# Attention with the scores turned round and their row maxima carried as operand rows

## The chip, the cores and the metric

One NeuronCore of a Trainium2 chip runs the whole kernel. The metric is the device time of one execution, in microseconds (us). The engines have their own instruction queues and run at the same time: TensorE (PE, and PEld for its weight loads), VectorE (DVE), ScalarE (ACT), GpSimd (POOL) and SyncE (SP), which here issues all the transfers (DMA).

## The reference, cut to what matters

Four batches of twelve heads, 448 tokens, head width 64. q and k are normalised by their root mean square; then comes softmax attention; its output, 1792 tokens of width 768, goes through a soft mixture of eight experts and then a gated product. All data are float32.

```python
q_n, k_n = (rmsnorm(q, g_q), rmsnorm(k, g_k))          # (4, 12, 448, 64)
scores = scale * np.matmul(q_n, k_n.transpose(0, 1, 3, 2))
scores = scores - np.max(scores, axis=-1, keepdims=True)
attn = np.exp(scores)
attn = attn / (np.sum(attn, axis=-1, keepdims=True) + 1e-09)
return np.matmul(attn, v).astype(np.float32)
# then: x = soft mixture of experts (phi, w1, w2) of x;  out = (x @ w_a) * (x @ w_b) @ w_out
```

## The kernel before

The kernel has three stages. Stage 1 is the attention, with the mixture's routing logits for each batch done between its steps. Stage 2 streams the weights of the eight experts, and stage 3 the gated product's weights and the final products. Weights travel in units of 1536 KB: nine of the fifty are loaded during stage 1, seven more as stage 1's buffers come free, the rest as stage 2 and 3 use them up.

Stage 1 goes over 24 *pairs* of heads (two heads fill the 128 partitions). For each pair:

- `load_qk`, `load_v`: three transfers from HBM. `square` (two a pair, on POOL except for the first pairs), `sumsq` (DVE) and `rsqrt` give the reciprocal roots: a logarithm and an exponential on ACT, then three small DVE steps (lines 288 to 292) that refine them. These steps have all their operands in SBUF. `normalise` (POOL) multiplies.
- `emit_T`: eight PE transposes put q and k with the head width on the partitions. ACT copies them out rounded to the short form (`et[:, 0]`, `et[:, 1]`, the high parts) and DVE subtracts to get the low parts.
- `emit_Z`: six transfers from SBUF to SBUF stack high and low parts of one head on 128 partitions, as `z`, so that two matmuls give a product of nearly full precision. There are four `z` tiles, one a head, so the tiles of one head come free as soon as that head's four steps are done.
- Eight *steps*, one for each head and each chunk `c` of 112 queries: `score` (two matmuls over `z`, 448 keys wide, queries on the partitions, then a DVE maximum over the keys, line 360), `expo` (ACT exponential with that maximum as its bias, and the sum over the keys as its accumulator, read out by a second instruction), `ptrans` (four PE transposes that put the keys on the partitions, line 382, and a copy out on ACT, line 388, or DVE, line 386).
- A pair later, `av`: four times two heads' matmuls of `pt` with `v`, accumulated in the PSUM tile `psv`; `spread` and `bcast` (a POOL copy, four PE transposes and an ACT copy) lay the reciprocal sums out over the head width, and `finish` multiplies.

The order of stage 1 is written by hand: a loop of 24 pairs times 8 steps, in which `score` runs two steps ahead and `expo` one. `moe_tasks` (routing logits and accumulation, per batch) are handed out one at a time in steps 3, 6 and 7. Only DVE's order is left to the framework's scheduler in stage 1. The weight units go in after `emit_Z` in step 6 of every second pair from the sixth on. `warm` puts dummy matmuls on PE while it would be idle.

Of the kernel before, what the change touches and what calls it, by code (L numbers as in the profile page):

```python
# [32 lines left out]
def kernel(  # L33
# [33 lines left out]
    P1_ENGINES = {ET.PE, ET.Activation, ET.Pool, ET.SP}  # L67
# [6 lines left out]
    W0 = 22  # L74
    WE = 7
# [73 lines left out]
    def tok_softmax(s, tp, pt):  # L149

        ps = pt("pslt")[0:P, 0:128]
        for c in range(NC):
            pe.matmul(
                ps[:, c * 32:(c + 1) * 32], s["l4"][:, c * P:(c + 1) * P], i4, start=True, stop=True
            )
        p3 = ps.rearrange("p (c s) -> p c s", s=32)
        m = tp.tile([P, 2, 4], F32, tag="cm", name="cm", bufs=1)
        ct = tp.tile([P, 4, 32], F32, tag="ct", name="ct", bufs=1)
        bc = lambda a: a.unsqueeze(2).to_broadcast([P, 4, 32])
        dve.tensor_reduce(out=m[:, 0, :], in_=p3, axis=AX.X, op=ALU.max)  # L160
        dve.tensor_tensor(out=ct, in0=p3, in1=bc(m[:, 0, :]), op=ALU.subtract)
        act.activation(out=ct, in_=ct, func=AF.Exp)
        dve.tensor_reduce(out=m[:, 1, :], in_=ct, axis=AX.X, op=ALU.add)
        dve.tensor_scalar(out=m[:, 1, :], in0=m[:, 1, :], scalar1=EPS, scalar2=None, op0=ALU.add)
        dve.reciprocal(out=m[:, 1, :], in_=m[:, 1, :])
        dve.tensor_tensor(out=ct, in0=ct, in1=bc(m[:, 1, :]), op=ALU.mult)
        s["ct"] = ct

    def tok_transpose(s, b, tp, pt):

        ps = pt("psct")[0:64, 0:S]
        c2 = tp.tile([P, 4, 2, 32], F32, tag="c2", name="c2", bufs=1)
        dve.tensor_copy(out=c2, in_=s["ct"].unsqueeze(2).to_broadcast([P, 4, 2, 32]))
        for c in range(NC):
            pe.transpose(
                ps[:, c * P:(c + 1) * P], c2[:, c].rearrange("p a s -> p (a s)"), ident[0:P, 0:P]
            )
        act.activation(out=cT[:, b, :], in_=ps, func=AF.Copy)
        dve.tensor_tensor(
            out=cT[32:64, b, :], in0=ps[32:64, :], in1=cT[32:64, b, :].bitcast(F32), op=ALU.subtract  # L180
        )
# [9 lines left out]
    with ExitStack() as c1:  # L191
# [4 lines left out]
        ep = c1.enter_context(tc.tile_pool(name="ep", bufs=1))  # L196
        one = c1.enter_context(tc.tile_pool(name="one", bufs=1))
        sqp = c1.enter_context(tc.tile_pool(name="sqp", bufs=2))
        one_ = c1.enter_context(tc.tile_pool(name="one_", bufs=1))
        pp = c1.enter_context(tc.tile_pool(name="pp", bufs=2))  # L200
        ptp = [c1.enter_context(tc.tile_pool(name="ptp0", bufs=2))]
        vp = c1.enter_context(tc.tile_pool(name="vp", bufs=2))
        sm = c1.enter_context(tc.tile_pool(name="sm", bufs=2))
        ptp.append(c1.enter_context(tc.tile_pool(name="ptp1", bufs=2)))
        ps_s = c1.enter_context(tc.tile_pool(name="ps_s", bufs=3, space=PSUM))
        ps_p = c1.enter_context(tc.tile_pool(name="ps_p", bufs=2, space=PSUM))
        ps_v = c1.enter_context(tc.tile_pool(name="ps_v", bufs=1, space=PSUM))
        ps_m = c1.enter_context(tc.tile_pool(name="ps_m", bufs=2, space=PSUM))
        EVAC_DVE = (1, 5)
        T0A, T0B, T0Z = 5, 6, 6  # L210
        TA, TB, TZ = 4, 5, 6

        NZ = 4
        zt = {(2 * NPAIR + i) % NZ: (one if i < 2 else one_).tile([128, 3, S], F32R, name=f"z{i}") for i in range(NZ)}

        qk_t, n_t, v_t, rinv_t, ssq_t, e_t, pt_t, av_t, xT_t = {}, {}, {}, {}, {}, {}, {}, {}, {}
        ps_of, p_of, nm_of, den_t, bc_t = {}, {}, {}, {}, {}
        NSTEP = 8 * NPAIR

        def load_qk(p):  # L220
            if p >= NPAIR:
                return
            b, hp = divmod(p, HP)
            t = qk_sb[0:P, p % 3 * 1024:(p % 3 + 1) * 1024].rearrange("p (i h x) -> p i h x", i=2, h=2)
            for i, src in enumerate((q, k)):
                sp.dma_start(out=t[:, i], in_=src[b, 2 * hp:2 * hp + 2].rearrange("h (p c) d -> p h (c d)", c=NC))
            qk_t[p] = t

        def load_v(p):
            if p >= NPAIR:  # L230
                return
            b, hp = divmod(p, HP)
            src = v[b, 2 * hp:2 * hp + 2].rearrange("h (p c) d -> p h c d", c=NC)
            if p < NPAIR - 1:
                t = vp.tile([P, 2, NC, D], F32, tag="v", name=f"v{p}")
                sp.dma_start(out=t, in_=src)
                v_t[p] = [t[:, hd] for hd in range(2)]
            else:
                x = tk.tile([128, S], F32, tag="l4", name="v23a", bufs=1)[0:P, 0:NC * D]
                y = tk.tile([P, 4, 2, 32], F32, tag="c2", name="v23b", bufs=1)  # L240
                v_t[p] = x.rearrange("p (c d) -> p c d", d=D), y.rearrange("p c (a e) s -> p c (a e s)", a=2)
                for hd in range(2):
                    sp.dma_start(out=v_t[p][hd], in_=src[:, hd])

        sq_t = {}

        def square(p, i, eng=None):
            if p >= NPAIR:
                return
            sq = sqp.tile([P, 512], F32, tag="sq", name="sq")  # L250
# [5 lines left out]
            sq_t[p, i] = sq  # L256

        def sumsq(p, i):
            if p >= NPAIR:
                return  # L260
# [6 lines left out]
        small = []  # L267

        def tick(n=1):
            for _ in range(n):  # L270
                if small:
                    small.pop(0)[1]()

        def rsqrt(p):

            if p >= NPAIR:
                return  # L280
            x = ssq_t.pop(p).rearrange("p a c -> p (a c)")
            y = sm.tile([P, 2, 8], F32, tag="rinv", name=f"rinv{p}", bufs=3)
            yf = y.rearrange("p a c -> p (a c)")
            t = sm.tile([P, 16], F32, tag="nt", name="nt", bufs=2)
            rinv_t[p] = y
            act.activation(out=t, in_=x, func=AF.Ln, bias=ssq_eps[0:P])
            act.activation(out=yf, in_=t, func=AF.Exp, scale=-0.5)
            small.append((p, lambda: dve.scalar_tensor_tensor(
                out=t, in0=yf, scalar=-0.5, in1=yf, op0=ALU.mult, op1=ALU.mult)))
            small.append((p, lambda: dve.scalar_tensor_tensor(  # L290
                out=t, in0=x, scalar=D * 1e-6, in1=t, op0=ALU.add, op1=ALU.mult)))
            small.append((p, lambda: dve.scalar_tensor_tensor(
                out=yf, in0=t, scalar=1.5, in1=yf, op0=ALU.add, op1=ALU.mult)))

        def normalise(p, eng=None):
            if p >= NPAIR:
                return
            assert not any(x[0] == p for x in small)
            n_t[p] = npp.tile([P, 2, NC, 2, D], F32, tag="n", name=f"n{p}")
            for i in range(2):  # L300
# [4 lines left out]
                        [P, 2, NC, D]  # L305
                    ),
                    op=ALU.mult,
                )
            qk_t.pop(p)

        def emit_T(p, i):
# [911 lines left out]
```

## Time and profile before

| | us |
|---|---|
| median of three runs | 589.34 (588.32 to 589.79) |
| the profiled execution, its own time | 591.54 |
| its span, first to last instruction | 589.6 |
| mean granted clock of TensorE | 0.985 of full speed |

A row of a profile gives the engine, the line of the kernel, the operation, the tiles written and read, and times. A timeline row begins with the start and the duration in us. Durations of matmuls contain the way through the array, so for the throughput of PE the reader should look at the distance between starts.

### The profile page before, as it was taken

How to read it: one execution, taken by the hardware profiler on the slowest of the kernel's cores; microseconds unless marked ns; L12 is line 12 of the kernel's file. 1: busy time of each engine (PE TensorE's matmuls, PEld its weight loads, DVE VectorE, ACT ScalarE, POOL GpSimd, SP SyncE). 2: the span in 40 equal slices, each digit the busy share in tenths (PEclk: the TensorE clock that was granted, in tenths of full speed). 3: DMA queues.
4: the chain of work that ended last, by engine and by line, in shares of the span. 5: the costliest groups of instructions: out<-in, count | busy, mean ns of one | idle time of the engine just before them, and what ended most of it. 6: DMA issues, size and time to landing. Idle time of an engine off the chain costs nothing.

```text
span 589.6 us, 10977 instructions
## 1 busy us (share of the span) xinstructions
PE 555.9 (94%) x3982; PEld 367.2 (62%) x3982; DVE 350.7 (59%) x703; ACT 360.3 (61%) x845; POOL 114.1 (19%) x136
## 2 busy tenths in 40 slices
PE   5889999999999999999999999888999999999997
PEld 5756555566665565655656545333675665689996
DVE  5777777768787677786677522122248878742211
ACT  4577787787787787877868720111279889442210
POOL 1233443333343433333110000001100000200000
PEclk8798999999999999999999999999999999999999
DMA  7956577797877978697769688999999991002332
GB/s 177 221 137 145 142 167 166 192 266 203 206 226 170 265 169 242 164 270 159 219 167 282 245 342 343 430 425 427 423 422 423 425 424 63 1 28 80 97 91 82
DMA packets 39574, 134.51 MB, mean 228 GB/s; under 512 B 5857, under 2 KB 25313, under 8 KB 33121
## 3 DMA queue, kind: packets, MB, share of 16 engines
q1 hardware_dynamic: 39520, 133.81, 72.0%
q8 instruction: 32, 0.52, 0.4%
q14 instruction: 22, 0.17, 0.1%
HBM read 95.26 MB, written 5.51 MB: 171 GB/s over the span
## 4 chain that ended last, share of the span: by engine, by line
PE 76%; DMA 8%; DVE 5%; ACT 4%; SPq 2%; issue 2%; ACTq 0%; DVEq 0%
PE psv L396 12%; PE pspt L382 12%; PE pss L358 6%; PE pss L359 5%; DMA z<-e 5%; PE psM L938 4%; PE psh L697 4%; PE pso L1138 3%; PE pso L1140 3%; PE pso L1139 3%; PE psS L721 3%; PE pst L325 3%; DMA wu_w<-in_moe_w_dram 2%; PE psS L938 2%; PE psx L509 2%
## 5 line engine op out<-in xcount | busy, mean ns | idle before, releaser
L360 DVE TENSOR_REDUCE nmx<-pss 112x1 f32<-112x448 f32 x192 | 118.6, 620 | 41.9 <-PE pss L359 41.5
L382 PEld LDWEIGHTS pspt<-ident,p 112*112 112x112 f32 x768 | 81.3, 135 | 79.7 <-ACT pt L388 28.9
L369 ACT ACTIVATE p<-pss,nmx 112x448 f32<-112x448 f32 x192 | 123.8, 645 | 10.1 <-DVE nmx L360 7.2
L382 PE MATMUL pspt<-ident,p 112*112 112x112 f32 x768 | 110.9, 267 | 2.9 <-ACT p L369 2.8
L388 ACT COPY pt<-pspt 112x448 f32<-112x448 f32 x144 | 76.9, 534 | 27.6 <-PE pspt L382 26.1
L396 PE MATMUL psv<-pt,v 112*64 112x448 f32 x368 | 90.3, 569 | 0.0
L358 PE MATMUL pss<-z 128*112 128x448 f32 x192 | 85.8, 447 | 0.0
L301 POOL TENSOR_TENSOR n<-xw,rinv 112x512 f32<-112x512 f32 x46 | 47.1, 1044 | 177.0 <-PE pst L325 112.1
L359 PE MATMUL pss<-z 128*112 128x448 f32 x192 | 70.9, 369 | 0.0
L386 DVE COPY pt<-pspt 112x448 f32<-112x448 f32 x48 | 29.9, 623 | 20.7 <-PE pspt L382 20.7
L255 POOL TENSOR_TENSOR sq<-xw 112x512 f32<-112x512 f32 x40 | 40.9, 1042 | 4.9 <-DMA xw<-in_q_dram 4.8
L369 ACT ACTIVATION_READ_ACCUMULATOR p<-pss,nmx 112x1 f32 x192 | 40.0, 208 | 0.0
L1138 PE MATMUL pso<-Mh,t 128*128 128x384 f32 x112 | 38.1, 340 | 0.5 <-DVE Ml L967 0.5
L358 PEld LDWEIGHTS pss<-z 128*112 128x112 f32 x192 | 34.4, 179 | 6.7 <-issue 5.8
L1140 PE MATMUL pso<-Mh,t 128*128 128x384 f32 x112 | 37.8, 337 | 0.0
L1139 PE MATMUL pso<-Ml,t 128*128 128x384 f32 x112 | 37.8, 337 | 0.0
L325 PE MATMUL pst<-ident,n 112*128 112x112 f32 x192 | 27.1, 267 | 11.2 <-ACT rd L427 6.0
L1157 DVE COPY ot<-pso 128x384 f32<-128x384 f32 (+1 forms) x14 | 7.6, 544 | 49.9 <-PE pso L1142 49.9
L396 PEld LDWEIGHTS psv<-pt,v 112*64 112x64 f32 x368 | 18.3, 135 | 29.6 <-issue 22.5
L359 PEld LDWEIGHTS pss<-z 128*112 128x112 f32 x192 | 34.5, 180 | 0.7 <-issue 0.6
L938 PE MATMUL psM<-w,G 128*128 128x512 f32 x64 | 33.8, 610 | 0.8 <-DVE G L901 0.8
L263 DVE TENSOR_REDUCE ssq<-sq 112x8 f32<-112x512 f32 x48 | 32.4, 677 | 2.7 <-ACT sq L253 2.3
(177 smaller groups left out, 878.0 us busy)
## 6 DMA issues: line engine op xcount, KB each, us to landing
wu_w<-in_moe_w_dram SPq DMA_DIRECT2D x38, 1536.0 KB, 13.5
z<-e SPq DMA_DIRECT2D x48, 336.0 KB, 4.6
z<-e SPq DMA_DIRECT2D x48, 224.0 KB, 4.4
r<-in_moe_w_dram SPq DMA_DIRECT2D x7, 1536.0 KB, 8.4
xw<-in_moe_w_dram SPq DMA_DIRECT2D x4, 1536.0 KB, 15.2
xw<-in_q_dram SPq DMA_DIRECT2D x24, 224.0 KB, 4.4
xw<-in_k_dram SPq DMA_DIRECT2D x24, 224.0 KB, 4.0
z<-e SPq DMA_DIRECT2D x48, 112.0 KB, 4.4
```

The source lines that it names most:

```text
L301: (eng if eng and i == 0 else pool).tensor_tensor(out=n_t[p][:, i].rearrange("p c h d -> p h c d"), in0=qk_t[p][:, i].rearrange("p h (c d) ...
L358: pe.matmul(ps, x, z[:, 1, :], start=True, stop=False)
L359: pe.matmul(ps, x, z[:, 2, :], start=False, stop=True)
L360: dve.tensor_reduce(out=nm_of[n // 8][:, h % 2, c:c + 1], in_=ps, axis=AX.X, op=ALU.max, negate=True)
L369: act.activation(out=t, in_=ps_of.pop(n), func=AF.Exp, bias=nm_of[n // 8][:, h % 2, c:c + 1], accum_out=den_t[n // 8][:, h % 2, c:c + 1],)
L382: pe.transpose(ps[:, kc * P:(kc + 1) * P], src[:, kc * P:(kc + 1) * P], ident[0:P, 0:P])
L388: act.copy(out=o, in_=i)
L396: pe.matmul(av_t[p][hd * D:(hd + 1) * D, 0:S], v_t[p][hd][:, kc, :], pt_t[2 * p + hd][:, kc, :], start=(kc == 0), stop=(kc == NC - 1),)
L938: pe.matmul(o, G[:, r], W[:, c], start=st, stop=sp_)
L1138: pe.matmul(o, ch[:, m], Mh[:, m, c], start=(m == 0), stop=False)
L1139: pe.matmul(o, ch[:, m], Ml[:, m, c], start=False, stop=False)
L1140: pe.matmul(o, cl[:, m], Mh[:, m, c], start=False, stop=False)
```

## The change

Only stage 1 changes.

- **Scores are transposed.** `score(p, kc, hd)` now puts 112 keys on the partitions and the 448 queries along the row, so the exponential's output is already what `av` needs. `ptrans` and its copies are gone, and so is the read of the accumulator.
- **The maxima come from one pass of their own.** `peak(p, c)` multiplies only the high parts, straight from the tile `e`, one matmul a head on its own 64 partitions, both heads into a two-bank PSUM tile; `peak_out` takes both heads' maxima in one DVE instruction over 896 columns. `rows(p)` transposes the maxima (four transposes of two columns) and `rows_out` (ACT) writes them into rows 64 and 65 of `z`'s fourth plane. The second matmul of `score` runs over 66 rows, and a row of ones (`fill_ones`, once) makes it add the maxima. The exponential then needs no bias.
- **The sums come from the exponentials.** `addup` on POOL adds the four key chunks of both heads (three additions of 896 columns a pair), `den` multiplies them with a matrix of ones (two float32 matmuls), `den_ln`, `den_exp` (ACT) and `den_test`, `den_step` (DVE) invert, and `finish` multiplies. `rden`, `spread` and `bcast` go.
- **Small operands in PSUM.** `root` writes one of two copies of its result, and `newton` its intermediate, into the unused columns 448 and up of the PSUM bank in which `av` accumulates (`bank`, `spare_ps`); `tok_softmax` keeps its four sums there too.
- **Squares shared.** One of the two squares of each pair goes from POOL to ACT (`SQ_ACT`).
- **Split operands of two pairs in turn.** `e` gets two buffers; `z` becomes two tiles of one whole pair each, in place of four of one head. Their number of transfers stays at six a pair, with the same bytes.
- **The order comes from a planner.** Every operation gets a cost, a due time (`p * T0 + OFF[kind]`), its dependencies and the buffers that it takes and gives; a list scheduler works out the order of all five engines. DVE's order in stage 1 is now fixed by it as well. The planner holds a transfer pair `Z` to 2.2 us of issue for a head and 4.0 us to land.

```diff
-    P1_ENGINES = {ET.PE, ET.Activation, ET.Pool, ET.SP}
+    P1_ENGINES = {ET.PE, ET.Activation, ET.Pool, ET.SP, ET.DVE}
+    SQ_ACT = (1,)
+    NPT, T0, MSTEP, WU0, WUS, MF, = 5, 11.5, 3.2, 4, 2, 13
...
-        ep = c1.enter_context(tc.tile_pool(name="ep", bufs=1))
+        ep = c1.enter_context(tc.tile_pool(name="ep", bufs=2))
...
+        zt = [zp[i].tile([128, 2, 4, S], F32R, name=f"z{i}") for i in range(2)]
+        bank = ps_v.tile([128, 512], F32, name="psv")
+        spare_ps = lambda n, w: bank[0:P, S + n:S + n + w]
...
+        def root(p):
             t = sm.tile([P, 16], F32, tag="nt", name="nt", bufs=2)
+            act.activation(out=t, in_=ssq_t[p].rearrange("p a c -> p (a c)"), func=AF.Ln, bias=ssq_eps[0:P])
+            act.activation(out=spare_ps(0, 16), in_=t, func=AF.Exp, scale=-0.5)
+            act.activation(out=t, in_=t, func=AF.Exp, scale=-0.5)
...
+            if s == 0:
+                dve.scalar_tensor_tensor(out=t, in0=spare_ps(0, 16), scalar=-0.5, in1=y, op0=ALU.mult, op1=ALU.mult)
...
+        def stack(p, hd):
+            z = zt[p % 2][:, hd].bitcast(F32)
+            src = e_t[p][hd * D:(hd + 1) * D].bitcast(F32)
+            sp.dma_start(out=z[0:D, 0:3], in_=src[:, QH:KL + 1])
+            sp.dma_start(out=z[D:128, 0:2], in_=src[:, QL:KH + 1:2])
+            sp.dma_start(out=z[0:D, 3], in_=src[:, QH])
...
+        def peak(p, c):
+            for hd in range(2):
+                r = slice(hd * D, (hd + 1) * D)
+                pe.matmul(ps[:, hd], et[r, QH, c * P:(c + 1) * P], et[r, KH, :], start=True, stop=True)
+        def peak_out(p, c):
+            dve.tensor_reduce(out=nm_t[p][:, c, :], in_=ps_of[p, "x"], axis=AX.X, op=ALU.max, negate=True)
...
+        def score(p, kc, hd):
+            pe.matmul(ps, z[:, 1, c], z[:, 0, :], start=True, stop=False)
+            pe.matmul(ps, z[0:66, 2, c], z[0:66, 3, :], start=False, stop=True)
+        def expo(p, kc, hd):
+            act.activation(out=pt_t[p, kc][:, hd, :], in_=ps_of.pop((p, kc, hd)), func=AF.Exp)
+        def addup(p, kc):
+            pool.tensor_tensor(
+                out=sum_t[p], in0=pt_t[p, 0] if kc == 1 else sum_t[p], in1=pt_t[p, kc], op=ALU.add
+            )
...
+        lim = {"qk": 3, "v": 2, "sq": 2, "n": 1, "m": 2, "e": 2, "z": 2, "x": 1, "nm": 2, "s": 3, "pt": NPT, "sum": 1,
...
+                op("SP", 2.2, o("Z", hd), ("Z", p, hd), lambda hd=hd: stack(p, hd), [("L", p, 0), ("L", p, 1)] + ([("Z", p, 0)] if hd else []), () if hd else ("z",))
+                op(None, 4.0, 0, ("z", p, hd), None, [("Z", p, hd)])
...
+                    op("PE", 0.44, o("S", x), ("S", p, kc, hd), lambda kc=kc, hd=hd: score(p, kc, hd),
+                       [("RW", p), ("z", p, hd)], ("s",), (("z", ("Z", p, 0)),) if (kc, hd) == (NC - 1, 1) else ())
...
+            op("SP", 0.6, (WU0 + WUS * x) * T0, ("wu", x), lambda x=x: load_unit(
+                None if x < NRING else 0 if x == NRING else extra),
+               [("S", WU0 + WUS * x, 0, 0)] + ([("wu", x - 1)] if x else []))
```

## Rows read from the trace of the kernel before

**Rows 1.** The page: busy time of PE, and the slices of PE and DMA.

```profile
PE 555.9 (94%) x3982; PEld 367.2 (62%) x3982; DVE 350.7 (59%) x703; ACT 360.3 (61%) x845; POOL 114.1 (19%) x136
...
PE   5889999999999999999999999888999999999997
...
DMA  7956577797877978697769688999999991002332
```

**Rows 2.** Busy time by stretch; at the end PE clock, DMA share, GB/s.

```profile
75.00:102.00 27.00, 25.30 (x163) 15.15 (x163) 19.07 (x42) 21.23 (x60) 10.80 (x12) 1.00 0.70 164
...
130.00:157.00 27.00, 26.61 (x180) 16.67 (x180) 21.60 (x51) 21.60 (x61) 9.35 (x10) 1.00 0.83 215
...
347.00:356.00 9.00, 8.80 (x66) 6.05 (x67) 3.63 (x10) 2.49 (x7) 0.56 (x2) 1.00 0.79 304
356.00:500.00 144.00, 134.49 (x1305) 79.36 (x1304) 68.75 (x119) 75.28 (x93) 7.03 (x13) 0.99 0.92 383
```

**Rows 3.** The tile z: durations min/median/max, first and last start; its transfers.

```profile
L358 PE MATMUL pss<-z x192: 363/437/717, 20.3 to 335.7; 128*112 128x448 f32 x192
...
DMA to landing us min/median/max: 3.4/4.4/6.8
```

**Rows 4.** Timeline of PE: two steps of one pair, and the first scores.

```profile
20.80 0.36 PE L358 MATMUL pss<-z 128*112 128x448 f32 x1
...
21.00 0.37 PE L359 MATMUL pss<-z 128*112 128x448 f32 x1
...
247.03 0.43 PE L358 MATMUL pss<-z 128*112 128x448 f32 x1
247.31 0.37 PE L359 MATMUL pss<-z 128*112 128x448 f32 x1
247.60 0.97 PE L396 MATMUL psv<-pt,v 112*64 112x448 f32 x4
248.51 0.60 PE L382 MATMUL pspt<-ident,p 112*112 112x112 f32 x4
248.87 0.43 PE L358 MATMUL pss<-z 128*112 128x448 f32 x1
249.15 0.36 PE L359 MATMUL pss<-z 128*112 128x448 f32 x1
249.35 0.55 PE L382 MATMUL pspt<-ident,p 112*112 112x112 f32 x4
249.66 0.44 PE L358 MATMUL pss<-z 128*112 128x448 f32 x1
```

**Rows 5.** Groups of the page: count, busy us, mean ns, idle before.

```profile
L360 DVE TENSOR_REDUCE nmx<-pss 112x1 f32<-112x448 f32 x192 | 118.6, 620 | 41.9 <-PE pss L359 41.5
...
L388 ACT COPY pt<-pspt 112x448 f32<-112x448 f32 x144 | 76.9, 534 | 27.6 <-PE pspt L382 26.1
...
L255 POOL TENSOR_TENSOR sq<-xw 112x512 f32<-112x512 f32 x40 | 40.9, 1042 | 4.9 <-DMA xw<-in_q_dram 4.8
```

**Rows 6.** SP's queue: a weight unit, and one pair's six stacking transfers.

```profile
141.98 0.60 SPq L139 DMA_DIRECT2D wu_w<-in_moe_w_dram  x1
...
150.49 0.47 SPq L343 DMA_DIRECT2D z<-e  x1
...
154.55 1.53 SPq L345 DMA_DIRECT2D z<-e  x1
```

**Rows 7.** Timeline: a small DVE step beside POOL's multiplications, and one alone.

```profile
17.34 0.17 DVE L288 SCALAR_TENSOR_TENSOR nt<-rinv 112x16 f32<-112x16 f32 x1
...
18.70 2.05 POOL L301 TENSOR_TENSOR n<-xw,rinv 112x512 f32<-112x512 f32 x2 [5.08 <-DVE rinv L292]
...
19.75 1.03 DVE L288 SCALAR_TENSOR_TENSOR nt<-rinv 112x16 f32<-112x16 f32 x1 [0.68 <-ACT rinv L287]
```

**Rows 8.** Timeline: the last pair's finish, and the product that opens stage 2.

```profile
346.37 0.62 DVE L437 TENSOR_TENSOR xT<-psv,rd 128x448 f32<-128x448 f32 x1 [6.27 <-PE psv L396]
...
356.01 1.42 PE L687 MATMUL psst<-wsel,acc 128*128 128x32 f32 x12
```

More of the change, by code (lines that the diff above doesn't have):

```diff
@@ L147, in release @@
             load_unit(p)
[L149 to L154, printed above, removed]
-            )
[L156 to L167, printed above, removed]
@@ L295, in normalise @@
[L295 to L300, printed above, removed]
-                (eng if eng and i == 0 else pool).tensor_tensor(
-                    out=n_t[p][:, i].rearrange("p c h d -> p h c d"),
-                    in0=qk_t[p][:, i].rearrange("p h (c d) -> p h c d", d=D),
-                    in1=rinv_t[p][:, i, :].rearrange("p (h c) -> p h c", h=2).unsqueeze(3).to_broadcast(
-                        [P, 2, NC, D]
-                    ),
-                    op=ALU.mult,
-                )
-            qk_t.pop(p)
@@ new lines, in den, with den_ln, den_exp @@
+        def den(p):
+            ps = ps_of[p, "d"] = ps_m.tile([128, 512], F32, tag="m", name="psden")[:, 0:S]
+            for hd in range(2):
+                pe.matmul(ps[hd * D:(hd + 1) * D], ones, sum_t[p][:, hd, :], start=True, stop=True)
+        def den_ln(p):
+            rd_t[p] = sm.tile([128, S], F32, tag="rd", name="rd", bufs=1)
+            act.activation(out=rd_t[p], in_=ps_of[p, "d"], func=AF.Ln, bias=eps)
+        def den_exp(p):
+            act.activation(out=rd_t[p], in_=rd_t[p], func=AF.Exp, scale=-1.0)
@@ new lines, in xt_copy, with accum @@
+            def xt_copy(c, h):
+                x = s["xs", c, h]
+                if h == 1 and c >= 2:
+                    dve.tensor_copy(out=x, in_=s["x", c, h])
+                else:
+                    act.copy(out=x, in_=s["x", c, h])
+                s["x", c, h] = x
+            def accum(h):
+                ps = s["a", h] = mt("psacc")[:, 0:HD]
+                for c in range(NC):
+                    pe.matmul(ps[c * 32:(c + 1) * 32, :], s["et"][:, c, :], s["x", c, h], start=True, stop=True)
@@ new lines @@
+        order, start, end = plan()
+        free, tail = 0.0, max(start[names["S", NPAIR - 1, x, 1]] for x in range(NC))
+        ps_w = []
+        for i in order:
+            if ops[i][0] == "PE":
+                gap = start[i] - free
+                if free and gap > 0.8 and start[i] <= start[names["S", 0, 0, 0]]:
+                    warm(ps_of["w"], int(WF * gap / 0.22))
+                elif gap > 0.8 and start[i] > tail + 4:
+                    if not ps_w:
+                        ps_w.append(ps_x.tile([128, 2, 512], F32, tag="x", name="warm")[:, 0])
+                    warm(ps_w[0], int(WF * gap / 0.22))
+                free = end[i]
+            if ops[i][3]:
+                ops[i][3]()
```

759 lines of the change are left out of this document (401 added, 358 removed).

## The prediction

> **What bounds the kernel now.** I read the page first: PE is busy for 94% of the span, and its slices stand at 8 or 9 from the third to the last, while the slices of DMA are near 9 only from the 25th to the 33rd [rows 1]. Then the busy times by stretch. In a stretch of the attention PE fills 25.3 to 26.6 of 27 us at full clock, ACT and DVE 19 to 22, POOL about 10, and the 16 DMA engines 70% without weight units and 83% with them. From 356 to 500 us the DMA moves 383 GB/s at a share of 92%: there the kernel waits for weights [rows 2]. So stage 1 is set by PE and stage 2 by transfers that start to run without a break once the first expert frees its weights. In stage 1 only nine units go in, and seven more while it ends; these sixteen do not depend on how long it lasts. What stage 1 gains is therefore given on, us for us, as long as its last buffers come free in the same order against its end; the DMA share of 79% from 347 to 356 us [rows 2] says that a few us of delay of one unit find room.
>
> Third, the pace. The first score starts at 20.3 us, the last at 335.7 [rows 3]; with 0.6 us for its own two matmuls, 24 pairs take 316 us, 13.17 us a pair, the mixture's tasks included. Fourth, PE's timeline, by starts. Two steps take 2.63 us, 247.03 to 249.66: a score 0.57 before `av` and 0.48 before transposes, `av` 0.91, four transposes 0.36 and 0.31 [rows 4]. Four such rounds are 10.5 us a pair; two `emit_T` and `bcast`, three sets of four transposes like these, make 1.0, and the rest to 13.17, 1.65 us, is the mixture and waiting. I put the waiting at 0.4.
>
> **The change on PE, a pair.** It takes away 4 × (0.36 + 0.31) = 2.68 us of `ptrans` and 0.33 of `bcast` [rows 4]. Scores now come in twos with one passage to and from float32 work instead of two. Back to back, matmuls of a score start 0.20 apart, and 0.27 to 0.29 beside other work [rows 4]; two scores then cost 0.28 + 0.20 + 0.20 + 0.29 = 0.97 against 1.05, so 0.3 us less for four rounds. Together 3.3 us go.
>
> It adds `rows`, four transposes, 0.36; `den`, two float32 matmuls of the width of one `av`, 0.91 [rows 4]; and the peaks, which no row shows. A peak of one chunk is two matmuls of 448 columns, each of which would take 0.20 alone [rows 4]. Below: both heads together take the time of one, 0.20. Above: one after the other with a passage on both sides, 0.28 + 0.29. I take 0.30, since the two heads use different halves of the partitions and write different banks, as the two heads of `av` use different halves of the output: four of those matmuls in 0.91 [rows 4]. Four chunks are 1.2 us, between 0.8 and 2.3. The sum added is 2.47, and PE's work falls by 0.86 us a pair, between 1.26 less and 0.24 more.
>
> The Trainium skill (TensorEngine Tiling (Array Packing), Key Properties) says that tiles of the array run independently, and also that a change of the tiling mode drains the array; by the first half a chunk of peaks would cost the lower bound, by the second nearer the upper. No run here shows row halves.
>
> **The other engines, a pair.** DVE loses eight maxima (118.6/24 = 4.9 us), and gains four over twice the columns. Twice 0.62 is the upper bound and 0.62 the lower [rows 5]; I take 1.1, 4.4 in all. It also gains `den_test` and `den_step`, two passes like a maximum, 1.2 us, and loses a third of the copies. It stays under its present 21.5/27 × 13.2 = 10.5 us a pair [rows 2]. ACT loses six copies of 0.53 (76.9/24 = 3.2 us) [rows 5] and eight accumulator reads, and gains a square, `rows_out`, `den_ln` and `den_exp`, four passes of about that length: it falls. POOL loses a square, 1.04, and the copy of `spread`, and gains three additions of 896 columns. By the square of 512 columns one is 1.04 × 896/512 = 1.82 [rows 5]: 5.5 us more, 8.7 in all, from about 4.6 [rows 2]. None of the three becomes the bound by its sum; their cover is that PE has more than 11 us to do.
>
> DMA's bytes stay. Its 0.70 × 13.17 = 9.2 us a pair without units, and 10.9 with [rows 2], stand in a shorter pair: 87% of 12.5 us. That is below the 92% of stage 2 but no longer far.
>
> The small steps in PSUM: with both operands in SBUF such a step took 0.17 us alone and 1.03 beside a POOL multiplication [rows 7]. Three a pair, on an engine that is not the bound, are worth nothing by themselves; with POOL twice as busy they would have begun to cost, and the move buys that off.
>
> **Waits.** The orders that matter are PE's. New ones: four times a maximum behind a peak (one two-bank buffer), the maxima behind `rows` and ACT's `rows_out` ahead of a pair's scores, the sum chain (addition, `den`, two ACT passes, two DVE passes) ahead of `finish`, which frees the bank for the next pair's `av`. Each has the better part of a pair to run in. The waits of before on the copies out of `pspt` (27.6 us idle on ACT alone [rows 5]) go. The tightest new one is `z`. Before, one head's tile was free after half a pair; now both heads' six transfers can start only when the last score two pairs back is done, and must land before the first score of their pair, one pair later. On SP they take 150.49 to 156.1, and the last lands 4.4 us after its start at 154.55 (median): 8.5 us [rows 3, 6]. A weight unit, 1.57 MB at 383 GB/s, is 4.1 us more [rows 2]. Its due time puts it, in every second pair from the fifth on, between the first head's transfers and the second's; SP also carries q, k and v behind them. That makes 12.6 us, just the length of a pair, and PE stands still for up to 1 us in those eight pairs. I allow 0.2 us a pair over the present waits for this and the rest: 13.17 − 0.86 + 0.19 = 12.5 us a pair.
>
> **The ends.** At the start the chain to the first score gets longer: the four peaks and maxima one behind the other, 4 × (0.3 + 1.1 + 0.3 for two hand-overs), `rows` and `rows_out`, about 8.5 us, beside the stacking transfers, which took the same 8.5. Filling the ones costs ACT four passes of 0.5 while the first q arrives. I take 1.5 us later. At the end, the last score to the last `finish` took 346.99 − 336.3 = 10.7 us [rows 3, 8]; now it is an exponential, an addition, `den`, two ACT and three DVE passes, 0.53 + 1.82 + 0.91 + 1.06 + 1.86 and seven hand-overs of 0.2, 7.6 us. I take 2.5 us less, as PE also has the mixture's first product in there. From there to the product that opens stage 2, 9 us [rows 8], the chain is the same.
>
> **The sum.** 24 × (13.17 − 12.5) = 16.1, less 1.5, plus 2.5: 17 us. The profiled execution would go from 591.54 to 574.5; it stands 2.2 us above the median of the runs, so the time would be 589.34 − 17 = 572.3 us.
>
> **The rivals.** First, the waits go and the peaks of two heads do run together: PE's 12.77 less 1.26 is 11.5, DMA's 10.9 does not let every second pair below about 11.8, and I put the pair at 12.0: 24 × 1.17 + 1 = 29 us, 560 us. For it speaks that PE is nearly without gaps now [rows 2]; against it, that this was a fixed alternation and the new order holds only as well as its costs.
>
> Second, `z` arrives late in most pairs, not only in those with a unit: v, q and k of 672 KB go ahead of it, and the pair settles at 13.0. It gives 24 × 0.17 + 1 = 5 us, 584 us. Against it, their place on SP is now behind `z`.
>
> Third, the shared bank, the one that ends slower. `root` and the three `newton` steps touch the bank of `av`. If accesses by different engines to one bank are kept apart, a step waits for the `av` in progress (0.97 us [rows 4]), and the next `av` on PE, with every score behind it, waits for the step, which stands on DVE behind a maximum of 1.1 us. One such wait a pair is about 1.1 us: 13.4 to 13.6 a pair, 24 × 0.4 − 1 = 9 us more, 598 us. It decides from 0.9 us a pair, where it eats what PE saves. For it: four touches within about 1.5 us, and an `av` about every 3 us, so half of the pairs meet one. Against: a wait on DVE costs only when PE comes up to it in order. The Trainium skill (PSUM — Partial Sum Buffer, PSUM bank collisions raise a hardware error) asks just this, to guard by bank and quadrant and not by address; no row of before shows two engines in one bank of stage 1.
>
> Fourth, the saving is used up by waits of all kinds, each small: no change, 589 us.
>
> **How the numbers follow.** Forecast 0.46 (564 to 580), first rival 0.20, second 0.14, third 0.14, fourth 0.06. A measurement here can tell about 0.3%, 1.8 us, from no change. Faster: 0.46 + 0.20 + 0.14 = 0.80, less 0.03 for second-rival cases that end at nothing, 0.77; same 0.06; slower 0.17. The range goes from 558, just under the first rival, to 591; it leaves out the third and the fastest part of the first.
>
> **What will show it.** Right: scores over about 300 us from start to start, two peaks' starts under 0.05 us apart, no gap of PE at the first score of a pair beyond 1 us, DVE below PE, `wu` followed by a late `z` at most. Wrong: PE's weight loads idle on `z` (second rival), on a `newton` step (third), or on a maximum; a maximum of 896 columns well over 1.1 us; additions on POOL near 2.3 us, which would bring POOL past 10 us a pair and the sum chain onto the path; or a stage 2 that begins earlier and still ends at the old time, since a buffer of stage 1 came free late.

## The result, and the profile after

The changed kernel takes 586.60 us (median of 10 runs, 584.11 to 597.99) beside 590.73 for the kernel before on the same chip (10 runs, 588.32 to 592.53). The ratio is 0.9915, with a 95% interval of 0.989 to 0.9941: about 5 us faster, where 17 were forecast. Some kernels below scatter by several per cent from run to run, with a lower mean clock in the longer runs (here 0.990 at 584.11 us and 0.964 at 597.99), so ratios are made from the runs of each kernel that lie near its fastest.

The profiled execution took 587.84 us with a span of 586.1. First the page: PE's busy time, and the slices of PE, of its granted clock and of DMA.

```profile
PE 557.8 (95%) x3564; PEld 326.8 (56%) x3564; DVE 333.9 (57%) x556; ACT 319.1 (54%) x607; POOL 231.4 (39%) x167
...
PE   8799999999999899999999999898999999999997
...
PEclk9999999999999599999999998999999999999999
DMA  6598699969899378999684869999999991002332
```

Beside [rows 1], PE issues 418 matmuls less and is busy for about 2 us more. One slice of the clock, the 14th, stands at 5; POOL has doubled. Then the stretches of [rows 2], with three of four microseconds around that slice. The columns are the length and the busy time of PE, PEld, DVE, ACT and POOL, then the granted clock, DMA's share and its GB/s; the share counts transfers by where they start, so it can pass 1.

```profile
75.00:102.00 27.00, 26.25 (x128) 11.77 (x127) 21.45 (x37) 20.09 (x44) 21.56 (x16) 1.00 1.05 259
130.00:157.00 27.00, 26.86 (x147) 12.94 (x145) 21.54 (x36) 19.28 (x41) 19.58 (x13) 1.00 0.95 230
188.00:192.00 4.00, 1.77 (x12) 0.79 (x8) 1.68 (x3) 1.32 (x3) 2.99 (x2) 0.95 1.07 204
192.00:196.00 4.00, 3.69 (x10) 1.02 (x10) 1.85 (x5) 1.70 (x6) 0.09 (x1) 0.50 0.76 159
200.00:204.00 4.00, 4.00 (x13) 2.40 (x10) 0.92 (x4) 1.71 (x5) 3.08 (x2) 0.50 0.00 0
347.00:356.00 9.00, 7.61 (x68) 5.16 (x70) 2.39 (x7) 0.66 (x3) 0.56 (x2) 0.81 0.57 215
356.00:500.00 144.00, 134.46 (x1294) 78.07 (x1287) 71.37 (x123) 77.43 (x97) 7.37 (x14) 0.99 0.91 381
```

In an undisturbed stretch PE is full, at full clock. Between 188 and 192 us it stands still for 2.2 us, and then it is busy again but at half clock (1.2 GHz). Next the tile z, to be held against [rows 3]: scores with first and last start, and the stacking transfers.

```profile
L346 PE MATMUL pss<-z x192: 361/450/716, 29.6 to 332.5; 128*112 128x448 f32 x192
...
DMA to landing us min/median/max: 3.4/6.0/10.6
```

The last score comes 3.2 us earlier than before, but the first one 9.3 us later: 302.9 us lie between them in place of 315.4. The copy of sT, the mixture's accumulated tokens with which stage 2 opens, gives the third mark; this is it before, then after.

```profile
357.51 0.32 ACT L688 COPY sT<-psst 128x192 f32<-128x192 f32 x1 [4.87 <-PE psst L687]
```

```profile
352.86 0.32 ACT L796 COPY sT<-psst 128x192 f32<-128x192 f32 x1 [5.02 <-PE psst L795]
```

These marks, first score, last score, sT and the end of the span, split the time into the terms of the forecast. The figures are differences to the profile before, with its span of 589.6. Two variants tried below stand beside it: one with only the place of the weight units changed, one with the start mended as well.

| gain in us | forecast | after | units behind only | units behind, early start |
|---|---|---|---|---|
| first to last score | 16.1 | 12.5 | 19.7 | 20.3 |
| ahead of the first score | -1.5 | -9.3 | -9.8 | -1.7 |
| last score to sT | 2.5 | 1.4 | 1.7 | 1.7 |
| after sT | 0 | -1.1 | 0.0 | 0.1 |
| sum | 17.1 | 3.5 | 11.6 | 20.4 |

**Where the start went.** The timeline of the kernel after, ACT and PE, from the first small step to the first score:

```profile
9.50 0.19 ACT L262 ACTIVATE psv<-nt 112x16 f32<-112x16 f32 x1 [1.68 <-PE psv L201]
...
10.62 4.96 PE L201 MATMUL psv<-ident 128*128 128x128 f32 x42 [1.23 <-DVE rinv L274]
15.41 0.55 PE L293 MATMUL pst<-ident,n 112*128 112x112 f32 x4
...
26.73 1.16 PE L201 MATMUL psv<-ident 128*128 128x128 f32 x8 [1.26 <-ACT psv L262]
27.82 0.46 PE L324 MATMUL psx<-e 64*112 64x448 f32 x2
28.21 0.55 PE L334 MATMUL psnm<-ident,nmx 112*2 112x112 f32 x4
...
29.58 0.45 PE L346 MATMUL pss<-z 128*112 128x448 f32 x1
```

L201 writes the dummy products that keep PE busy at the start, and it writes them into psv, the bank in which the small steps of root and newton now lie. ACT waits 1.68 us for dummies; PE's next dummies wait 1.23 us for DVE's step; then 42 of them, by the profile's count, take 4.8 us ahead of the first transposes.

**Where the clock went.** The same view at the stop: POOL, ACT and PE.

```profile
189.01 1.04 POOL L250 TENSOR_TENSOR sq<-xw 112x512 f32<-112x512 f32 x1 [3.78 <-DMA xw<-in_q_dram]
...
190.34 0.63 ACT L248 ACTIVATE sq<-xw 112x512 f32<-112x512 f32 x1 [2.88 <-DMA xw<-in_k_dram]
...
192.07 0.19 ACT L262 ACTIVATE psv<-nt 112x16 f32<-112x16 f32 x1
...
192.31 1.76 PE L365 MATMUL psv<-pt,v 112*64 112x448 f32 x4 [2.53 <-ACT psv L262]
```

And SP's queue ahead of it, as in [rows 6]:

```profile
175.62 0.61 SPq L143 DMA_DIRECT2D wu_w<-in_moe_w_dram  x1
176.28 0.47 SPq L315 DMA_DIRECT2D z<-e  x1
...
180.03 0.32 SPq L236 DMA_DIRECT2D xw<-in_q_dram  x1
181.03 1.39 SPq L236 DMA_DIRECT2D xw<-in_k_dram  x1
```

In order of time: q and k are issued behind a weight unit and the second head's stacking transfers, and the square of q starts 9 us after q's issue, when q has landed. Root waits for the squares, and the next `av` on PE, which shares root's bank, waits for root. PE loses 2.5 us, and then works at half clock until about 205 us. For z, on the other hand, PE waits only 1.5 us in all pairs together, at most 0.9 at once.

**Other rows that the prediction named.** A peak and what follows it, to be held against [rows 4]; and groups, against [rows 5].

```profile
213.32 0.46 PE L324 MATMUL psx<-e 64*112 64x448 f32 x2
213.71 0.46 PE L346 MATMUL pss<-z 128*112 128x448 f32 x1
214.01 0.37 PE L347 MATMUL pss<-z 66*112 66x448 f32 x1
214.31 0.97 PE L373 MATMUL psden<-sum,ones 112*64 112x448 f32 x4
```

```profile
L329 DVE TENSOR_REDUCE nmx<-psx 112x2 f32<-112x896 f32 x96 | 104.5, 1088 | 31.2 <-PE psx L324 30.1
L357 POOL TENSOR_TENSOR sum<-sum,pt 112x896 f32<-112x896 f32 x48 | 100.6, 2096 | 13.2 <-ACT pt L352 11.2
```

The two heads of a peak do run at one time: two matmuls together take 0.46 us. But from the start of the peaks to the start of the next work a chunk costs 0.39, not 0.30. The maximum came as forecast (1.088 beside 1.1); the addition takes 2.10, not 1.82.

### The profile page after: what moved, and what is told of

Same layout as the page of the kernel before. It is cut to its first block, busy times and chain, and to the rows that moved or that the text cites. A ratio compares the mean times of both kernels' runs of the same rounds, so it can differ in the third digit from the quotient of the medians.

```text
span 586.1 us, 9656 instructions
## 1 busy us (share of the span) xinstructions
PE 557.8 (95%) x3564; PEld 326.8 (56%) x3564; DVE 333.9 (57%) x556; ACT 319.1 (54%) x607; POOL 231.4 (39%) x167
## 4 chain that ended last, share of the span: by engine, by line
PE 81%; DMA 7%; DVE 5%; ACT 4%; issue 1%; POOL 1%; SPq 1%; ACTq 0%; DVEq 0%; POOLq 0%
PE psv L365 12%; PE pss L346 8%; PE pss L347 6%; PE psx L324 5%; DMA z<-e 4%; PE psM L1046 4%; PE psh L805 4%; PE psS L829 4%; PE pso L1246 3%; PE pso L1248 3%; PE pso L1247 3%; PE psden L373 3%; PE pst L293 3%; PE psv L201 3%; DMA xw<-in_k_dram 3%; PE psL L201 2%
## 5 line engine op out<-in xcount | busy, mean ns | idle before, releaser
L352 ACT ACTIVATE pt<-pss 112x448 f32<-112x448 f32 x192 | 98.2, 541 | 49.8 <-PE pss L347 44.1
L329 DVE TENSOR_REDUCE nmx<-psx 112x2 f32<-112x896 f32 x96 | 104.5, 1088 | 31.2 <-PE psx L324 30.1
L357 POOL TENSOR_TENSOR sum<-sum,pt 112x896 f32<-112x896 f32 x48 | 100.6, 2096 | 13.2 <-ACT pt L352 11.2
L346 PE MATMUL pss<-z 128*112 128x448 f32 x192 | 83.0, 432 | 1.0 <-DMA z<-e 0.9
L347 PE MATMUL pss<-z 66*112 66x448 f32 x192 | 71.6, 373 | 0.6 <-DMA z<-e 0.6
L357 POOL TENSOR_TENSOR sum<-pt,pt 112x896 f32<-112x896 f32 x24 | 50.3, 2096 | 32.7 <-ACT pt L352 24.2
L346 PEld LDWEIGHTS pss<-z 128*112 128x112 f32 x192 | 34.0, 177 | 42.8 <-issue 20.3
L324 PE MATMUL psx<-e 64*112 64x448 f32 x192 | 44.2, 456 | 1.9 <-DVE nmx L329 1.6
L324 PEld LDWEIGHTS psx<-e 64*112 64x112 f32 x192 | 16.7, 170 | 48.4 <-DVE nmx L329 16.1
L365 PEld LDWEIGHTS psv<-pt,v 112*64 112x64 f32 x384 | 19.7, 137 | 31.5 <-issue 22.2
L347 PEld LDWEIGHTS pss<-z 66*112 66x112 f32 x192 | 34.4, 179 | 2.8 <-DMA z<-e 1.1
L908 ACT ACTIVATE top<-wu_w,few 128x1536 f32<-128x1536 int8 x18 | 31.4, 1746 | 0.4 <-DVE xw L926 0.4
L926 DVE SCALAR_TENSOR_TENSOR xw<-wu_w,top 128x768 int32<-128x768 int32 x24 | 22.2, 954 | 15.7 <-ACT top L912 15.7
```

The lines of the kernel that those rows point to most:

```text
L324: pe.matmul(ps[:, hd], et[r, QH, c * P:(c + 1) * P], et[r, KH, :], start=True, stop=True)
L329: dve.tensor_reduce(out=nm_t[p][:, c, :], in_=ps_of[p, "x"], axis=AX.X, op=ALU.max, negate=True)
L346: pe.matmul(ps, z[:, 1, c], z[:, 0, :], start=True, stop=False)
L347: pe.matmul(ps, z[0:66, 2, c], z[0:66, 3, :], start=False, stop=True)
L352: act.activation(out=pt_t[p, kc][:, hd, :], in_=ps_of.pop((p, kc, hd)), func=AF.Exp)
L357: pool.tensor_tensor(out=sum_t[p], in0=pt_t[p, 0] if kc == 1 else sum_t[p], in1=pt_t[p, kc], op=ALU.add)
```

## The experiments

**The dummies' bank.** All the variants start from the changed kernel.

```diff
-            ps = ps_of["w"] = bank
+            ps = ps_of["w"] = ps_s.tile([128, 512], F32, tag="s", name="warm")
```

> The changed kernel with its first dummy matmuls written into a bank of the scores instead of the bank of av, where the small operands of the roots lie; nothing else, same order. Theory A (the first score comes late because of the dummy matmuls: their bank makes ACT's write of the root and the small DVE steps wait, and they stand ahead of the first transposes): the write of the first root no longer waits 1.68 us and the dummy matmuls no longer wait 1.26 us for ACT; the first score moves from 29.5 to about 27, most of what the bank costs; the first transposes stay near 15. Rival B (the start is set by the peaks and their maxima and by the transfers): the first score stays at 29 to 30.

Measured: 585.85 us in one run; first score at 24.8, last at 326.8. The bank alone brings 4.8 us of the start. The stop at `av` is still there (2.47 us, up to 188 us), and 10.2 us at half clock follow it.

**No dummies ahead of the first transposes.**

```diff
-                if free and gap > 0.8 and start[i] <= start[names["S", 0, 0, 0]]:
+                if free and gap > 0.8 and start[i] <= start[names["S", 0, 0, 0]] and i != names["T", 0, 0]:
```

> The changed kernel without the 42 dummy matmuls ahead of the first pair's transposes; the others stay, in the bank of av. Theory A: the first transposes begin at about 12.3 us, when the first normalised q is there, instead of 15.4, and the first score comes about 3 us earlier, near 26.5. Rival B: the first score moves by less than 1 us, since the transfers or the maxima end last.

Measured: 582.92 us in one run; first score at 27.3, last at 325.5. The first transposes begin at 10.3 us. The stop at `av` is 1.06 us here, and no half clock follows. This run gains 2.3 us at the first score and 4.7 more by the last.

**Both edits of the start.**

> Both edits of the two runs before together. Theory A: first transposes at about 10.5 us, first score at 23 to 24 instead of 29.5, and since PE works nearly without gaps from the first score to the end of the attention, the whole time falls by as much: 5 to 6 us below the changed kernel, ratio to the kernel before 0.981 to 0.985. Rival B2 (what is gained at the start is lost again in the pairs, because the transfers or the sum chains set their pace): first score earlier, but the whole time within 2 us of the changed kernel, ratio 0.989 to 0.993.

Measured: first score at 22.2 us, as the sum of the two says, but 588.82 us (median of 580.03, 587.11, 590.53, 604.32); ratio 0.9871 (0.9795 to 0.9947). The forecast gain of the whole time is not shown. In the profiled run (590.53 us) the 7.4 us arrive at the first score and are gone by the last (333.1). There the longest stop is at a score that waits for its stacked queries:

```profile
79.00 0.42 PE L346 MATMUL pss<-z 128*112 128x448 f32 x1 [1.89 <-DMA z<-e]
```

These are the windows around it and behind it:

```profile
76.00:80.00 4.00, 2.02 (x12) 1.19 (x12) 1.62 (x2) 1.26 (x4) 1.75 (x1) 1.00 1.14 231
...
84.00:88.00 4.00, 4.00 (x12) 1.00 (x8) 2.98 (x5) 2.11 (x4) 3.12 (x4) 0.50 1.02 215
```

DMA's share is above 1 around the stop, and from about 81 to 105 us PE is at half clock although it is busy. Between its first and last score this run holds 27.3 us at half clock, the kernel after 13.7; half of the difference, 6.8 us, is most of what the early start loses again. So the start was the largest mis-sized term, and yet not the whole.

**The small operands in SBUF,** on top of the early start: `ssq`'s root and the newton steps read and write a tile of SBUF, as before the change, and not the spare columns of psv.

```diff
-        spare_ps = lambda n, w: bank[0:P, S + n:S + n + w]
+        smalls = sm.tile([P, 64], F32, name="spare", bufs=1)
+        spare_ps = lambda n, w: smalls[:, n:n + w]
```

> As the run before, and the small operands of the roots and of the token softmax in SBUF instead of the bank of av; same order. Theory C (the shared bank makes PE's av wait for ACT and DVE, and this is the 2.5 us stop near 190 us after which the clock was halved): no PE wait on ACT's root ahead of av, no stretch of the attention at half clock after its start, 3 to 5 us less than the run before; the small DVE steps beside POOL take about 1 us instead of 0.18, about 2 us of DVE a pair, which DVE has to spare. Rival D (what the move into PSUM bought off is worth more): DVE's waits on POOL pass on to the maxima and to PE; 2 us or more slower than the run before.

Measured: 613.48 us (median of 601.97, 611.31, 615.65, 631.5); its fastest run is 22 us above the fastest of the run before it. The theory that the shared bank costs more than it brings fell. The timeline of the profiled run (611.31 us) shows the direct effect in one pair: two of the small steps, each beside an addition on POOL, and between them one that was let through.

```profile
242.74 2.09 POOL L358 TENSOR_TENSOR sum<-pt,pt 112x896 f32<-112x896 f32 x1 [3.35 <-PE psden L374]
...
243.04 1.82 DVE L270 SCALAR_TENSOR_TENSOR spare<-spare,nt 112x16 f32<-112x16 f32 x1 [1.39 <-ACT nt L264]
...
244.90 0.17 DVE L272 SCALAR_TENSOR_TENSOR spare<-ssq,spare 112x16 f32<-112x16 f32 x1
244.91 4.27 POOL L358 TENSOR_TENSOR sum<-sum,pt 112x896 f32<-112x896 f32 x2
...
245.10 1.95 DVE L275 SCALAR_TENSOR_TENSOR rinv<-spare,nt 112x16 f32<-112x16 f32 x1
...
248.41 0.68 PE L553 MATMUL psx<-ident,xT 128*112 128x128 f32 x3 [2.12 <-DVE rd L389]
```

A step that takes 0.17 us alone waits out an addition of 2.1 us, where it waited out a multiplication of 1.03 in [rows 7]; the steps queued behind it on DVE come late, PE stands still for 2.12 us, and 248 to 252 us run at a clock of 0.58. In PSUM the first of these steps takes between 172 and 183 ns in all 24 pairs. In SBUF 16 of the 72 small steps take over 0.9 us, and all together 39.0 us in place of 12.8. But most of the time lost is clock: this run holds 64.8 us at half clock between its first and last score, where the early start's profile holds 27.3. The Trainium skill (SBUF — State Buffer, Who interferes with whom) says that a DVE instruction with two inputs in SBUF contends with a GpSimd instruction that reads SBUF, and one with at most one such input, outside DVE's two-port modes, doesn't; this run (1.82 and 1.95 us) and the kernel after (172 to 183 ns) agree with it.

**All squares on POOL,** on top of the early start.

```diff
-    SQ_ACT = (1,)
+    SQ_ACT = ()
```

> As e3_start, with both squares of a pair on POOL again, as before the change (the planner orders anew). Theory E (sharing the squares costs: k's square stands in ACT's queue, waits there for a late transfer of k, and ACT's root behind it holds up av on PE): no PE stop at av near 190 us, fewer stretches at half clock; 3 to 6 us less than e3_start. Rival F (POOL is near its limit with three additions of 2.1 us): POOL gets 1.04 us more a pair, about 9.5 to 10 in all, the sums come later, and the time is the same as e3_start or up to 5 us more.

Measured: 589.34 us (median of 10, 577.71 to 601.64), ratio 0.9804 (0.9765 to 0.9842). The interval overlaps that of the early start alone (0.9795 to 0.9947). In the profiled run (590.58 us) the stop at `av` near 190 us is gone, but other stops at `av` and at z remain, up to 1.5 us, with 20.5 us at half clock. Whether ACT's share of the squares matters stays open.

**Small operands in the peaks' bank,** on top of the early start: still in PSUM, but beside `psx`, not beside `av`.

```diff
-        spare_ps = lambda n, w: bank[0:P, S + n:S + n + w]
+        xbank = ps_x.tile([128, 2, 512], F32, name="psx2")
+        spare_ps = lambda n, w: xbank[0:P, 0, S + n:S + n + w]
...
-            ps = ps_of[p, "x"] = ps_x.tile([128, 2, 512], F32, tag="x", name="psx2")[0:P, :, 0:S]
+            ps = ps_of[p, "x"] = xbank[0:P, :, 0:S]
...
```

> As e3_start, with the small operands in the spare columns of the bank of the peaks instead of the bank of av; same order. Theory C2 (av and the small steps in one bank hold each other up: the DVE step that waits 1.5 us for av near 107 us, and av that waits 2.5 us for ACT near 190 us): both stops go, 2 to 5 us less than e3_start. Rival: the peaks' bank is no better, since peaks and maxima use it more often than av uses its own; more waits of ACT on the bank, time equal or longer.

Measured: 584.51 us (median of 577.83, 581.73, 587.28, 593.14), ratio 0.9806 (0.9759 to 0.9854). That can't be told from the early start alone. In the profiled run (593.14 us) the wait of `av` for root is gone, and PE's longest stops are 1.10 us at `den`, for an addition, and 1.05 at a score, for z. Half clock comes all the same, 44.3 us of it between the first and the last score. So the wait for root is not needed for it; whether the bank moves the time is not shown.

**q and k of four pairs in flight,** on top of the early start; the place comes from one unit that is loaded at the end.

```diff
-            t = qk_sb[0:P, p % 3 * 1024:(p % 3 + 1) * 1024].rearrange("p (i h x) -> p i h x", i=2, h=2)
+            t = xw[1 - p // 3 % 2][0:P, p % 3 * 1024:(p % 3 + 1) * 1024].rearrange("p (i h x) -> p i h x", i=2, h=2)
...
-        lim = {"qk": 3, ...
+        lim = {"qk": 4, ...
...
-        for x in range(NRING + 2):
+        for x in range(NRING + 1):
...
```

> As e3_start, with q and k of four pairs in flight instead of three (a second weight buffer lends its place, and its unit is loaded at the attention's end, so one unit less goes through the middle); the planner orders anew. Theory H (q and k come late because their buffer comes free late, a pair ahead of their square): ACT's and POOL's waits on q and k, 8.5 us of POOL and several of ACT in the changed kernel, go, and with them the stop at av near 190 us: 2 to 6 us less than e3_start. Rival G: q and k in time, yet the time within 2 us of e3_start, since the stops come from z or from the sharing of the bank.

Measured: 578.46 us (577.14 to 586.6), ratio 0.977 (0.974 to 0.98). By the ratios that is about 6 us below the early start alone, as forecast, but the intervals just overlap. The stop at `av` near 190 us is gone; one of 1.81 us for z, which ends at a score at 81.3 us, is left, with half clock from 81 to 91 us.

**The units behind both heads' stacking transfers,** on top of the early start.

```diff
-                [("S", WU0 + WUS * x, 0, 0)] + ([("wu", x - 1)] if x else []))
+                [("S", WU0 + WUS * x, 0, 0), ("Z", WU0 + WUS * x + 1, 1)] + ([("wu", x - 1)] if x else []))
```

> As e3_start, with each weight unit issued behind the transfers of both heads of its pair instead of between them; PE, DVE, ACT and POOL keep their order. Theory G (the unit between the two heads makes z late for PE): the PE stops at a pair's first score in pairs with a unit (near 77 and 270 us) go, and with the first of them the half clock that followed it; 2 to 8 us less than e3_start. Rival H (what is late is q and k, which a unit delays wherever it stands): the stop at av near 190 us stays or grows, and the time is within 2 us of e3_start.

Measured: 572.71 us (571.15 to 575.07), ratio 0.969 (0.9659 to 0.9721), the fastest of all. The page shows PE at 544.1 us of busy time in place of 557.8, and a clock without a dent in the pairs:

```profile
PE 544.1 (96%) x3522; PEld 317.1 (56%) x3522; DVE 334.8 (59%) x556; ACT 318.9 (56%) x607; POOL 231.3 (41%) x167
...
PE   7999999999999999999999989889999999999996
...
PEclk9999999999999999999999999989999999999999
DMA  6998799787989496998765959999999990013232
```

Its scores run from 22.0 to 317.1 us: 295.1, or 12.3 us a pair with the ends in it. PE waits 0.2 us for z in all, its longest stop between them is 1.4 us, behind a maximum, and the wait of `av` for root that cost 2.53 is 0.59:

```profile
183.12 0.97 PE L365 MATMUL psv<-pt,v 112*64 112x448 f32 x4 [0.59 <-ACT psv L262]
```

**The units behind, without the early start.**

> Only the place of the weight units is changed: each is issued behind the second head's stacking transfers of its pair, not between the two heads' ones; the late start of the kernel after the change (first score at 29.5 us) stays. If the late start and the units' place are two separate causes that add up, this is the 572.7 us of the run with both, plus the 7 us that the two edits of the start brought there to the first score (29.5 against 22.0): about 580 us, with no stretch at half clock between the first and the last score. Rival: the place of the units does nothing unless the start is early as well (the run with both was merely spared the stops): then it stays at 585 to 588 us, with a stop of PE of 2 us or more near the eighth or thirteenth pair and half clock behind it.

Measured: 580.58 us (579.73 to 582.12), ratio 0.9854 (0.9829 to 0.9879). That is what the first theory gave: with the units behind, the early start is worth 7.9 us (580.58 and 572.71) for the 8.1 by which its first score comes earlier. The two do not simply add up, though: with the unit between the heads the early start brought no clear gain (ratios 0.9915 without and 0.9871 with it, their intervals overlapping). And the profile holds a surprise. Moving the unit has hardly moved q, since a unit still stands ahead of q, and the stop at `av` is still there, 2.08 us; but the clock stays up:

```profile
188.70 1.04 POOL L250 TENSOR_TENSOR sq<-xw 112x512 f32<-112x512 f32 x1 [3.66 <-DMA xw<-in_q_dram]
...
191.67 0.60 PE L365 MATMUL psv<-pt,v 112*64 112x448 f32 x2 [2.08 <-ACT psv L262]
```

The window behind it:

```profile
192.00:196.00 4.00, 4.00 (x24) 1.99 (x22) 3.07 (x8) 2.67 (x6) 0.00 (x0) 1.00 0.30 75
```

Against the kernel after, its scores span 295.7 us in place of 302.9. Of these 7.2 us, 0.45 are the shorter stop; the rest, 6.75, agrees with what half clock takes: by the windows of the kernel after 0.4 us of it lie in 188 to 192, 12 up to 204 and 1.3 behind (a clock of 0.84 to 208), 13.7 in all, of which half, 6.85, is lost.

**Units behind, early start, and q and k of four pairs:** the last two edits together.

> The early start, the units behind both heads' stacking transfers, and q and k of four pairs in flight in place of three (one weight unit less is loaded during the pairs). Theory: both later edits remove waits for transfers that stand behind a unit, of the stacked queries and of q and k; once the units stand last, q and k wait for them still, but the run with the units behind showed only 0.96 us of such a stop, so this gains at most 1 to 2 us on its 572.7: 571 to 573. Rival: the unit that is loaded later is missed at the end of the pairs, where the experts already wait for transfers: 4 us later, 576 to 577.

Measured: 573.58 us (570.85 to 576.52), ratio 0.9734 (0.9686 to 0.9782): no gain over the units behind alone. Its profile has no half clock between the first and the last score, and neither has that of the units behind: q and k in time are worth little once the clock holds.

**Without the dummies of stage 2's opening,** on top of the early start and the units behind. The new order puts seven of them ahead of the mixture's last logits.

```diff
-    W4 = 7
+    W4 = 0
```

> The early start and the units behind both heads' stacking transfers, and the seven dummy products of the opening of stage 2, which the new order puts ahead of the mixture's last logits on TensorE, are left out. Theory: in the profile they take 1.65 us from start to start on the chain from the last finish to the copy of sT (327.32 to 328.97 in the run with both edits), about 1.3 us of it after the copy of the logits they could have waited for; without them the copy of sT starts 1.0 to 1.6 us earlier behind the last score (20.1 us there), and the time falls from 572.7 by as much, to about 571.5. Rival: the chain waits for something else in that place, or the following products run at a lower clock for the missing dummies: the copy of sT stays at 20 us behind the last score and the time at 572 to 574.

Measured: 572.75 us (571.52 to 575.23), ratio 0.9694 (0.9657 to 0.9731). The copy of sT comes 19.4 us behind the last score in place of 20.1, and the time stays. The products that follow are longer, at a lower clock (from 330 to 340 us it is 0.83, with the seven 1.00); `psst` and the next dummies, first with the seven and then without:

```profile
335.61 1.50 PE L795 MATMUL psst<-wsel,acc 128*128 128x32 f32 x12 [1.39 <-DVE wsel L791]
336.94 0.91 PE L201 MATMUL psL<-ident 128*128 128x128 f32 x6
```

```profile
335.12 1.86 PE L795 MATMUL psst<-wsel,acc 128*128 128x32 f32 x12 [1.39 <-DVE wsel L791]
336.79 1.63 PE L201 MATMUL psL<-ident 128*128 128x128 f32 x6
```

The theory was right on the chain and wrong on the time: in these two profiles the dummies gave back about what they cost, as the rival said. It is no rule: the kernel after has the seven too, and from 347 to 356 us its clock was 0.81.

## Why the prediction was off, step by step

**The direction, and PE's work per pair, were right.** With the units behind, a pair takes 12.3 us, a little under the forecast 12.5, and PE is what bounds it (290 of the 295.1 us busy). The removed passes, the maxima of 1.09 us and `den` at 0.97 came as reckoned. The peaks ran both heads at once but cost 0.39 a chunk, 1.56 us a pair in place of 1.2: inside the bounds, and too little to matter. POOL's additions at 2.10 us lie near the 2.3 named as a danger; they did not become the bound.

**The step that failed first is "The ends".** It took 1.5 us for the start, from the chain of peaks and maxima and the filling of the ones; the start measured 9.3. I had costed the steps that the change adds and not the dummy products that share a bank with them. The shared bank was my third rival, placed at `av` and DVE in every pair; there PE waited for it only once for long, 2.5 us, though DVE waited some 14 us for `av` under cover. It bit at the start: moving the dummies to another bank gives 4.8 us back, leaving out those ahead of the first transposes 2.3, and both 7.4. The Trainium skill (PSUM — Partial Sum Buffer, PSUM bank collisions raise a hardware error) asks for order by bank and quadrant and not by address; the trace agrees, with waits of 1.68 and 2.53 us between engines that touch different columns of psv.

**The second is "Waits".** It had weight units make z late, and allowed 0.2 us a pair, counting a stop at its own length. z did land later, in 6.0 us (median; [rows 3] has 4.4) and at most 10.6, but in the kernel after PE waited for it only 1.5 us in all. The stop that counted came from late q and k, by way of root and the shared bank, and late q and k had no term in the sum. What the step had at nothing is what a stop can bring after it: 2.5 us of standing came with 13.7 us at half clock, half of them lost, so that one stop cost 9 us.

How much that weighs can be estimated from the profiles. Take half of its time at half clock off each span from the first to the last score. The kernel before goes from 315.4 us to 312.0, since it holds 6.8 us of half clock too (its clock is 0.65 from 24 to 28 us and 0.71 from 44 to 48), which I had read as part of its pace. The kernel after goes from 302.9 to 296.0, and the eleven variants lie between 293 and 302. So at full clock the pairs would have gained 16 us, as forecast, and what parts the variants between their first and last score is mostly the clock.

The units' place alone is worth 3.6 us by the ratios (0.9915 and 0.9854), and 10.7 with the early start (0.9871, itself known only to 0.9795 to 0.9947, and 0.969). Transfers come late in these runs, as the rows of z, q and k show; why one stop drops the clock and another does not is not settled (below).

**Two errors of my working went unseen.** The moved small operands were costed at "nothing by themselves", with the remark that they "would have begun to cost" beside a busier POOL. In SBUF they cost some 22 us, beside the early start: this edit carries the others. And for the tail I forecast an unchanged chain behind the last finish; it grew by 1.9 us, from 10.5 (346.99 to 357.51) to 12.4 (340.47 to 352.86). These are the last finish and the seven dummies, which stood behind the mixture's work before and stand ahead of `pslr` now:

```profile
339.85 0.62 DVE L395 SCALAR_TENSOR_TENSOR xT<-psv,rd 128x448 f32<-128x448 f32 x1
```

```profile
342.70 1.82 PE L201 MATMUL psL<-ident 128*128 128x128 f32 x14
344.36 0.92 PE L515 MATMUL pslr<-l,i 128*128 128x448 f32 x2
```

They are part of that chain, but taking them away did not move the time.

**The sum.** In the table, the start is short by 7.8 us, the pairs by 3.6, the tail by 1.1, and 1.1 are lost behind sT, of which the lower clock up to 356 us can be a part: 13.6 of the 17.1 us. With both causes mended the same terms give 20.4, and the kernel takes 572.7 us. That the figures meet (572.3 and 572.7) is partly luck: the pairs are 4.2 us better than reckoned and the tail 0.8 worse, and the runs before stood 2 us higher on that chip.

## What to carry to other kernels

When an operand moves into a bank or a queue, list everything else that uses it, the filling work at the start included, and price the start as its own chain. Where PE is the bound, a transfer that may come late is to be priced with the half clock that can follow the stop, so what nobody waits for soon, such as a weight unit, goes behind all transfers of the pair. And an edit that looks free because another engine is idle should be tried at the new load of that engine.

## What the runs showed that I had not expected

Half clock came with or behind a stop of PE in some places and not in others, though PE was busy again at once: with 2.53 us in the kernel after (13.7 us at half clock), 2.47 with the dummies' bank moved (10 us), 1.89 with the early start (24 us), 1.81 with q and k of four pairs (10 us), and no more than 1.05 with the small operands in the peaks' bank (37 us, 78 to 115); but not with 2.08 us with the units behind only, nor with 1.06 without the dummies ahead of the transposes. The length of the stop alone does not decide it, and no run here separates what else does. Nor did I expect 2.10 us for an addition of 896 columns on POOL where a square of 512 takes 1.04: it is 15% more than in proportion.
